# A retention front moved off GpSimd, with scores on array quarters and small products on array halves

## The chip, the cores and the metric

The kernel runs on one NeuronCore of a Trainium2 chip. The metric is the device time of one execution in microseconds (us). Three runs of the kernel before gave 735.53, 735.69 and 737.09 us, median 735.69 us; this kernel's measurement can tell about 0.2% from no change. The engines are named as in the profile: PE (TensorE, matrix products), PEld (its weight loads), DVE (VectorE), ACT (ScalarE), POOL (GpSimd) and SP (SyncE, which here only starts transfers).

## The reference, cut to what matters

Three layers follow each other, all in fp32.

```python
# 1 retention: batch 2, heads 8, sequence 768, head width 64
state = gamma[h] * state + outer(k_t, v_t)        # gamma differs by head
y_t   = scale * (q_t @ state)                     # -> x: 1536 tokens x 512

# 2 mixture of 8 experts, one expert per token, at most `capacity` = 384 tokens each
expert = argmax(x @ w_gate, axis=1)
pos    = number of earlier tokens of the same expert
out[i] = gate_w[i] * relu(x[i] @ w1[expert]) @ w2[expert]     if pos < capacity, else 0

# 3 four experts that every token passes, weighted by normalised domain_probs
out = sum_e p[:, e] * (relu(x @ w1[e]) @ w2[e])
```

## The kernel before, in words

The kernel has a front (layer 1 and the routing of layer 2), then the products of layer 2, then those of layer 3. The change lies wholly in the front, which ends with the first expert product (line 950). All work is written out in program order; each engine takes its own instructions strictly in that order, and semaphores hold an instruction until what it reads is there and what it overwrites has been read.

The front works on 12 token tiles of 128 tokens (6 per batch entry), numbered 0 to 11 here. For a tile i it does:

- `st_v`: vg(i) = v times a decay factor per head and position, 128x512, on POOL (line 250). It needs the transfer kv(i).
- `st_S`: the scores S(i) = k q, 8 products of 64 rows and 128 columns (line 266), into two PSUM banks, then on DVE the causal mask, giving sd(i) (line 271).
- `st_I`, `st_U`, `st_O`: products with the carried state (line 309), the new state U (line 290, copied out by ACT, line 295), and the scores times vg (line 321). `st_I` and `st_O` add up in the same two banks.
- `st_x`: O(i) is copied out by ACT (line 335) and multiplied by the decay `gqs` on POOL (line 336) into xT(i), the tokens with features on partitions. For the last two tiles DVE does both in one step (line 340).
- `x_pe`: the token product X(i) (line 364), 4 products against `iw`, an identity with the gate's 8 columns beside it: this turns the tile to one token per partition and gives the gate logits at once. `x_reduce` then has DVE add up the logits (line 379), ACT copy the tokens out to `xk` (line 383), and ACT's queue write `xk` to DRAM, `xd` (line 387).
- `x_dve`: the argmax as a one-hot `ohs`, the running counts `cum`, and `ohk` (token number times one-hot), all small DVE instructions.
- `r_pe`, `r_dve`: the rank product R(i) (lines 349, 350) counts earlier tokens of the same expert; DVE picks the token's rank and makes the selection matrix `at` (line 439, 128x256).
- `g_pe`: the selection product (line 446) collects the token numbers per expert slot.

A loop over `it` from 0 to 11 sets the order: it does `st_I/U/O/x` of tile it-1, `st_v` of tile it+1, `st_S` of tile it, starts the transfers of tile it+3 (512 KB each for q with k, and for k with v; 256 KB of `gqs` in the first rounds), then `x_pe` of tile it-2, `g_pe` of it-4, `r_pe` of it-3. "Round it" below is one pass of this loop. At round 8 the first expert weight is split in two (`split_w(0)`: ACT line 141, then DVE line 142). After the loop stand the last tiles' remaining steps, the gather of the first expert's tokens, and products (lines 528, 536) that build its input.

PSUM has eight banks: four are handed out in turn to S, O and R, and four are fixed (`slot` for the selection, `u` for the state, `x0` and `x1` for the token product).

## Time and profile before

| | before |
|---|---|
| median of 3 runs | 735.69 us |
| profiled execution | 735.49 us, span 733.7 us, granted clock 0.999 |
| PE busy over the span | 722.3 us (98%) |
| DVE, ACT, POOL busy | 473.5, 339.0, 202.5 us |
| first expert product (line 950) starts | 68.46 us after the span's start |

The span runs from the first to the last instruction of the profiled execution; some 1.8 us of its own time lie around it. After 70 us PE is busy without a gap in every stretch, so the time of the front stands ahead of a rigid block. "PE busy" counts matmuls whose ends are modelled and overlap, so how dense PE really works is read from where the next group starts. Products of fp32 stand in the trace as two instructions each. [...]

### The profile page before, as it was taken

What the parts mean: (1) busy time and instruction counts of PE and PEld (TensorE: products, weight loads), DVE (VectorE), ACT (ScalarE), POOL (GpSimd) and SP (SyncE); (2) the same over time, 40 slices, a digit from 0 to 9 for tenths busy, and PEclk for the clock granted to TensorE, in tenths of its full rate; (3) what the DMA queues carried; (4) which work ended last, traced back from release to release, by engine and by line L of the source; (5) the groups of instructions that cost most, each with busy time, mean ns of one, the idle gap of its engine ahead of it and who ended that gap; (6) DMA issues with size and microseconds to landing.
All of it is one profiled execution on the core that took longest, in us unless ns stands there. A gap on an engine that the chain in (4) does not pass through costs nothing.

```text
span 733.7 us, 11338 instructions
## 1 busy us (share of the span) xinstructions
PE 722.3 (98%) x4425; PEld 657.2 (90%) x4426; DVE 473.5 (65%) x777; ACT 339.0 (46%) x545; POOL 202.5 (28%) x193
## 2 busy tenths in 40 slices
PE   8998999999999999999999999999999999999997
PEld 6887999999999888999889998889998899988896
DVE  3888899898898835545743655763475454557334
ACT  2344767676656533334433445633344334444331
POOL 3653854443044012212323111223422121111103
PEclk9999999999999999999999999999999999999999
DMA  9984886687741211211122122122222212112102
GB/s 331 414 338 138 287 320 220 228 281 245 230 144 34 89 55 59 86 58 58 61 91 78 38 77 87 59 85 88 87 72 71 92 53 86 59 58 79 37 1 86
DMA packets 28026, 92.83 MB, mean 127 GB/s; under 512 B 4097, under 2 KB 4369, under 8 KB 27970
## 3 DMA queue, kind: packets, MB, share of 16 engines
q1 hardware_dynamic: 23042, 81.79, 32.2%
q0 software_dynamic: 3056, 7.05, 2.8%
q10 hardware_dynamic: 1872, 3.24, 1.2%
q8 instruction: 35, 0.57, 0.3%
q14 instruction: 21, 0.17, 0.1%
HBM read 85.72 MB, written 6.34 MB: 125 GB/s over the span
## 4 chain that ended last, share of the span: by engine, by line
PE 88%; DVE 1%; POOL 1%; ACT 0%; issue 0%; POOLq 0%; ACTq 0%
PE o L1212 35%; PE a L1056 17%; PE m L950 15%; PE b L1056 9%; PE m L953 7%; PE bb L1056 5%; POOL out_dram L1224 1%; PE ab L1056 0%; DVE x L855 0%; DVE X L868 0%; ACT X L864 0%; DVE c L1149 0%; POOLq L1409 0%; ACT c L1087 0%; PE T L768 0%
## 5 line engine op out<-in xcount | busy, mean ns | idle before, releaser
L1212 PE MATMUL o<-w,g_c 128*128 128x512 f32 x1152 | 267.4, 390 | 0.0
L1212 PEld LDWEIGHTS o<-w,g_c 128*128 128x128 f32 x1152 | 215.9, 188 | 43.7
L142 DVE TENSOR_TENSOR w<-raw,w 128x1024 fp32r<-128x1024 f32 x128 | 158.4, 1247 | 13.9 <-ACT w L141 13.6
L1056 PE MATMUL a<-X,w 128*128 128x384 f32 x720 | 145.2, 336 | 0.0
L157 POOL TENSOR_TENSOR t<-raw 128x512 f32<-128x512 f32 x28 | 38.8, 1386 | 349.6 <-DMA raw<-b 302.2
L1091 DVE TENSOR_TENSOR c<-b,c 128x384 f32<-128x384 f32 x30 | 16.7, 558 | 181.1 <-PE b L1056 181.1
L141 ACT CAST w<-raw 128x1024 fp32r<-128x1024 f32 x128 | 132.1, 1047 | 2.5 <-DMA raw<-a 1.1
L1056 PEld LDWEIGHTS a<-X,w 128*128 128x128 f32 x720 | 127.5, 188 | 2.6 <-DVE c L1091 0.3
L1087 ACT COPY c<-a 128x384 f32<-128x384 f32 x60 | 28.8, 479 | 196.3 <-PE a L1056 196.3
L950 PE MATMUL m<-xet,w 128*128 128x448 f32 x256 | 80.8, 375 | 0.8 <-PEq L635 0.8
L1072 ACT ACTIVATE g_c<-c 128x384 fp32r<-128x384 f32 x96 | 50.4, 526 | 66.0 <-DVE c L1091 64.7
L950 PE MATMUL m<-h,w 128*128 128x448 f32 x256 | 80.8, 375 | 0.0
L1056 PE MATMUL b<-X,w 128*128 128x384 f32 x360 | 72.1, 334 | 0.0
L953 PE MATMUL m<-h,w 128*128 128x224 f32 x256 | 67.5, 264 | 0.0
L953 PE MATMUL m<-xet,w 128*128 128x224 f32 x256 | 67.5, 264 | 0.0
L624 POOL DMA_INDIRECT xe<-xd,gidx x42 | 53.7, 1278 | 47.3 <-DVE xT L752 35.7
L1056 PEld LDWEIGHTS b<-X,w 128*128 128x128 f32 x360 | 63.5, 188 | 0.0
L1076 DVE SCALAR_TENSOR_TENSOR g_c<-c,g_c 128x384 fp32r<-128x384 f32 x96 | 52.9, 552 | 3.9
L950 PEld LDWEIGHTS m<-xet,w 128*128 128x128 f32 x256 | 48.0, 187 | 4.6 <-PEq L635 1.0
L950 PEld LDWEIGHTS m<-h,w 128*128 128x128 f32 x256 | 48.0, 187 | 3.7
L953 PEld LDWEIGHTS m<-xet,w 128*128 128x128 f32 x256 | 48.9, 191 | 0.0
L953 PEld LDWEIGHTS m<-h,w 128*128 128x128 f32 x256 | 48.9, 191 | 0.0
(158 smaller groups left out, 766.7 us busy)
## 6 DMA issues: line engine op xcount, KB each, us to landing
raw<-a SPq DMA_DIRECT2D x64, 512.0 KB, 4.9
raw<-b SPq DMA_DIRECT2D x64, 512.0 KB, 3.5
qk<-qkv SPq DMA_DIRECT2D x12, 512.0 KB, 8.3
kv<-qkv SPq DMA_DIRECT2D x12, 512.0 KB, 8.1
xd<-xk ACTq DMA_DIRECT2D x12, 256.0 KB, 6.2
gqs<-gqt SPq DMA_DIRECT2D x6, 256.0 KB, 7.5
xe<-xd,gidx POOLq DMA_INDIRECT x44, 4.9
iw<-cst SPq DMA_DIRECT2D x1, 272.0 KB
```

The lines of the kernel that those rows point to most:

```text
L141: nc.scalar.copy(w[:, 0], r)
L142: nc.vector.tensor_tensor(out=w[:, 1], in0=r, in1=w[:, 0].bitcast(F32), op=ALU.subtract)
L157: eng.tensor_tensor(out=c[:, 0:2], in0=b[:, 2:4], in1=b[:, 1:3], op=sub)
L624: nc.gpsimd.indirect_dma_start(out=t[:, b], out_offset=None, in_=xq, in_offset=bass.IndirectOffsetOnAxis(ap=gidx[:, b, e:e + 1], axis=0),)
L950: nc.tensor.matmul(out=b2, lhsT=w[0], rhs=x, start=first, stop=last, skip_group_check=True)
L953: nc.tensor.matmul(out=b2[:, 0], lhsT=w[1], rhs=x[:, 0], start=False, stop=last, skip_group_check=True)
L1056: nc.tensor.matmul(out=bk[:, 0:HT], lhsT=w[:, sw, k], rhs=x[:, sx, k], start=(first and m == 0), stop=(m == len(steps) - 1), skip_group_ch ...
L1072: nc.scalar.activation(out=h2[:, 0], in_=src, func=AF.Relu)
L1076: nc.vector.scalar_tensor_tensor(out=h2[:, 1], in0=src, scalar=0.0, in1=h2[:, 0].bitcast(F32), op0=ALU.max, op1=ALU.subtract,)
L1087: nc.scalar.copy(t, bk[:, 0:HT])
L1091: nc.vector.tensor_tensor(out=t, in0=bk[:, 0:HT], in1=t, op=ALU.add)
L1212: nc.tensor.matmul(out=bk, lhsT=h2[:, sh, cols], rhs=w[:, sw, k], start=(q == 0 and m == 0 and (n, t) not in begun), stop=(m == 2), skip_g ...
```

## The change

- POOL leaves the front, except for vg(0) and vg(1). The other ten vg are made by ACT, in 8 instructions of 128x64 each, at the place in the program where POOL's stood. xT is made by DVE for all tiles, straight from PSUM. `ohk` moves from DVE to ACT.
- The scores are 16 products on 64x64 quarters of the array in place of 8 on 64x128. From round 4 on they stand at the head of the round, ahead of `st_I`.
- The token, rank and selection products are cut in halves of 64 array columns: 8, 4 and 4 products a round in place of 4, 2 and 2. The rank product writes into the spare end of the token product's bank and stands ahead of it.
- PSUM is dealt out in pairs of banks: one for S (`s2`), one for O (`o2`), one for X with R (`x`). The ring of four is gone.
- The logits are added up in one DVE instruction, the maximum is a second; `xk` is one ACT copy of 512 columns in place of two of 256. The selection compares against an fp16 table.
- The constant `iw` is no longer loaded whole (544 columns): an identity and the gate (160 columns) are loaded after kv(2), and ACT spreads them. kv(1) is started ahead of gq(0), kv(2) ahead of the constants.
- The steps after the loop stand in another order.

```diff
+    def two(tag, name):
+        return ps[0].tile([P, 2, 512], F32, tag=tag, name=name)
...
         def st_v(i):
...
+            v = kv[:, 1].rearrange("p (h d) -> p h d", h=8)
+            if i < 2:
+                nc.gpsimd.tensor_tensor(
...
+            else:
+                for h in range(8):
+                    nc.scalar.activation(
+                        out=vg[:, h], in_=v[:, h], func=AF.Copy, scale=gk[:, i % NCH, h:h + 1]
+                    )
...
         def st_S(i):
...
-            bks = [bank(f"S{i}_{j}") for j in range(2)]
+            s2 = two("s2", f"S{i}")
+            bks = [s2[:, j] for j in range(2)]
             for hp in range(4):
                 cols = slice(hp * P, (hp + 1) * P)
-                for j in range(2):
+                for m in range(4):
+                    o, j = 64 * (m >> 1), m & 1
                     r = slice(64 * j, 64 * j + 64)
                     nc.tensor.matmul(
-                        out=bks[j][:, cols], lhsT=qk[r, 1, cols], rhs=qk[r, 0, cols],
-                        start=True, stop=True,
+                        out=bks[j][o:o + 64, cols],
+                        lhsT=qk[r, 1, hp * P + o:hp * P + o + 64], rhs=qk[r, 0, cols],
...
         def st_x(i):
...
-            if i < NT - 2:
-                ot = p2.tile([P, 512], F32, tag="ot", name=f"ot{i}")
-                for j in range(2):
-                    nc.scalar.copy(ot[:, 256 * j:256 * j + 256], bks[j][:, 0:256])
-                nc.gpsimd.tensor_tensor(out=xT, in0=ot, in1=gqs[:, c], op=ALU.mult)
...
+            for j in range(2):
+                cols = slice(256 * j, 256 * j + 256)
+                nc.vector.tensor_tensor(
+                    out=xT[:, cols], in0=bks[j][:, 0:256], in1=gqs[:, c, cols], op=ALU.mult
+                )
...
+        def r_pe(i, bk):
+            for o in (0, 64):
+                half = bk[o:o + 64]
+                nc.tensor.matmul(
+                    out=half, lhsT=onesb[:, o:o + 64], rhs=cum[:, i], start=True, stop=False,
...
+        def x_pe(i, rank=None, reduce=True):
...
+            b2 = xbs[i] = two("s2" if i == NT - 1 else "x", f"X{i}")
+            if rank is not None:
+                r_pe(rank, b2[:, 1, 448:456])
+            for hp in range(KD):
+                for o in (0, 64):
+                    nc.tensor.matmul(
+                        out=b2[o:o + 64, hp // 2, hp % 2 * 256:hp % 2 * 256 + 136],
+                        lhsT=xT[:, hp * P + o:hp * P + o + 64], rhs=iw[:, hp], start=True,
...
-            yield nc.vector.tensor_scalar(
-                out=ohk[:, i], in0=ohs[:, i], scalar1=tok[:, i:i + 1], scalar2=None, op0=ALU.mult
+            yield nc.scalar.activation(
+                out=ohk[:, i], in_=ohs[:, i], func=AF.Copy, scale=tok[:, i:i + 1]
             )
...
         for it in range(NT):
+            if it >= EARLY_S:
+                st_S(it)
             if it >= 1:
                 st_I(it - 1)
...
-            st_S(it)
+            if it < EARLY_S:
+                st_S(it)
...
+            if it == 1:
+                eye = ig[:, 0:P].rearrange("p (k c) -> p k c", k=1).to_broadcast([P, KD, P])
+                nc.scalar.copy(iw[:, :, 0:P], eye)
+                nc.scalar.copy(iw[:, :, P:136], ig[:, P:XW].rearrange("p (k c) -> p k c", k=KD))
...
-                x_pe(it - 2)
+                x_pe(it - 2, it - 3 if it >= 3 else None)
...
         st_I(NT - 1)
-        x_pe(NT - 2)
-        r_pe(NT - 3)
         st_O(NT - 1)
-        braid(r_dve(NT - 3))
-        g_pe(NT - 4)
-        g_pe(NT - 3)
         st_x(NT - 1)
+        x_pe(NT - 2, NE - 1, False)
+        g_pe(NE - 2)
+        braid(r_dve(NE - 1))
+        g_pe(NE - 1)
```

On ACT, in round 2 of the kernel before, from the state copy of tile 1 to the write of tile 0's tokens (`ot` is the copy of O(1), `xk` that of X(0)):

```order
L295 COPY st_114<-U_173 128x256
L335 COPY ot_244<-O_0_216 128x256
L335 COPY ot_244<-O_1_217 128x256
L383 COPY xk_270<-X_0_272 128x2x4x32
L383 COPY xk_270<-X_1_273 128x2x4x32
L387 DMA xd<-xk_270 128x512
```

The same place on ACT in the changed kernel (`kv_178` is the transfer kv(3)):

```order
L311 COPY st_116<-U_181 128x256
L265 ACTIVATE vg_267<-kv_178,cdec 128x64 x8
L397 COPY xk_304<-X_305 128x4x4x32
L401 DMA xd<-xk_304 128x512
L423 ACTIVATE ohk<-ohs,kc 128x8
```

The eight instructions that need kv(3) now stand ahead of the copy that empties X(0)'s banks; before they stood on POOL's queue.

On PE, in the kernel before, from the last score product of round 5 to the first state product of round 6 (`S` are scores, `O` what `st_I` and `st_O` write, `slot_ps` the selection):

```order
L266 MATMUL S_1_490<-qk_263 128x128
L364 MATMUL X_0_509<-iw,xT_398 128x136 x2
L364 MATMUL X_1_510<-iw,xT_398 128x136 x2
L446 LDWEIGHTS at_449
L446 MATMUL slot_ps<-ohk,at_449 128x8
L446 LDWEIGHTS at_449
L446 MATMUL slot_ps<-ohk,at_449 128x8
L349 LDWEIGHTS onesb
L349 MATMUL R_523<-cum,onesb 128x8
L350 LDWEIGHTS ub
L350 MATMUL R_523<-ohs,ub 128x8
L309 MATMUL O_0_537<-qk_263,st_115 64x128
```

On PE in the changed kernel, round 5 from its start up to its token product:

```order
L281 MATMUL S_515<-qk_296 64x128 x16
L326 MATMUL O_534<-qk_231,st_116 64x128 x8
L306 MATMUL U_181<-vg_354,kv_234 64x64 x8
L338 MATMUL O_534<-sd_417,vg_354 64x128 x8
L361 LDWEIGHTS onesb
L361 MATMUL X_579<-cum,onesb 64x8
L365 LDWEIGHTS ub
L365 MATMUL X_579<-ohs,ub 64x8
L361 LDWEIGHTS onesb
L361 MATMUL X_579<-cum,onesb 64x8
L365 LDWEIGHTS ub
L365 MATMUL X_579<-ohs,ub 64x8
```

The scores went from between O and X to the head of the round, next to the state product that also uses quarters, and the rank product went ahead of X into X's own tile.

## Rows read from the trace of the kernel before

**Rows 1.** Busy us (instructions) of PE, PEld, DVE, ACT, POOL; granted clock, DMA share, GB/s.

```profile
40.00:50.00 10.00, 10.00 (x168) 8.88 (x167) 8.28 (x33) 4.68 (x13) 4.83 (x5) 1.00 1.03 415
...
70.00:80.00 10.00, 10.00 (x68) 9.59 (x67) 8.60 (x13) 6.14 (x12) 7.87 (x8) 1.00 0.86 286
```

**Rows 2.** The chain that ended last, 0 to 70 us: start, length, what.

```profile
67.88 0.58 issue
68.46 0.44 PE m L950
```

**Rows 3.** Timeline of PE, a round: start, length, line, op, out<-in.

```profile
42.16 0.67 PE L309 MATMUL O<-qk,st 64*64 64x128 f32 x16
42.76 0.69 PE L290 MATMUL U<-vg,kv 128*64 128x64 f32 x16
43.28 1.10 PE L321 MATMUL O<-sd,vg 128*64 128x128 f32 x16
44.30 1.16 PE L266 MATMUL S<-qk 64*128 64x128 f32 x16
45.40 1.19 PE L364 MATMUL X<-iw,xT 128*128 128x136 f32 x8
46.43 0.20 PE L446 MATMUL slot_ps<-ohk,at 128*128 128x8 f16 x2
46.48 0.17 PE L349 MATMUL R<-cum,onesb 128*128 128x8 f16 x1
...
46.60 0.32 PE L309 MATMUL O<-qk,st 64*64 64x128 f32 x1
```

**Rows 4.** Timeline of PE, rounds 3 and 4.

```profile
17.70 1.16 PE L266 MATMUL S<-qk 64*128 64x128 f32 x16
18.79 1.19 PE L364 MATMUL X<-iw,xT 128*128 128x136 f32 x8
...
22.23 1.16 PE L266 MATMUL S<-qk 64*128 64x128 f32 x16
23.32 1.20 PE L364 MATMUL X<-iw,xT 128*128 128x136 f32 x8
```

**Rows 5.** Timeline of POOL: vg(2), vg(3), vg(4); in brackets the idle time before.

```profile
15.05 1.04 POOL L250 TENSOR_TENSOR vg<-kv,cdec 128x512 f32<-128x512 f32 x1 [3.01 <-DMA kv<-qkv]
...
19.59 1.04 POOL L250 TENSOR_TENSOR vg<-kv,cdec 128x512 f32<-128x512 f32 x1 [2.26 <-PE X L364]
...
22.93 1.04 POOL L250 TENSOR_TENSOR vg<-kv,cdec 128x512 f32<-128x512 f32 x1 [1.06 <-DMA kv<-qkv]
```

**Rows 6.** Groups by line and form, 0 to 56 us: busy, mean ns | idle before.

```profile
L383 ACT COPY xk<-X 128x256 f32<-128x256 f32 x19 | 6.2, 375 | 17.1 <-DVE lgs L379 17.1
...
L397 DVE SCALAR_TENSOR_TENSOR cd<-lgs,mxs,kc 128x8 f32<-128x8 f32 x9 | 4.5, 496 | 0.3
...
L446 PEld LDWEIGHTS <-at 128*128 128x128 f16 x16 | 1.6, 98 | 0.1
...
L141 ACT CAST w<-raw 128x1024 fp32r<-128x1024 f32 x1 | 1.0, 1045 | 0.9 <-DMA kv<-qkv 0.9
```

**Rows 7.** Timeline of PE, the scores of round 7.

```profile
35.31 1.16 PE L266 MATMUL S<-qk 64*128 64x128 f32 x14 [0.35 <-DVE ranks L424]
```

**Rows 8.** Timeline of DVE, rounds 8, 9 and after.

```profile
44.95 1.23 DVE L142 TENSOR_TENSOR w<-raw,w 128x1024 fp32r<-128x1024 f32 x1 [0.79 <-ACT w L141]
46.09 1.28 DVE L271 TENSOR_TENSOR sd<-S,cdec 128x512 f32<-128x512 f32 x2
...
53.52 0.76 DVE L340 TENSOR_TENSOR xT<-O,gqs 128x256 f32<-128x256 f32 x2
...
56.29 0.23 DVE L397 SCALAR_TENSOR_TENSOR cd<-lgs,mxs,kc 128x8 f32<-128x8 f32 x1
```

**Rows 9.** Timeline of PE, after the loop.

```profile
54.49 1.19 PE L364 MATMUL X<-iw,xT 128*128 128x136 f32 x8
...
68.46 0.44 PE L950 MATMUL m<-xet,w 128*128 128x448 f32 x1 [0.83 <-PEq L635]
```

More of the change, by code (lines that the diff above doesn't have):

```diff
@@ L75, in tile_retention_moe_moe, with one, bank @@
     ps = [sctx.enter_context(tc.tile_pool(name="ps", bufs=1, space=PSUM))]
-    banks = [f"bank{n}" for n in range(4)]
-    held = ["slot", "u", "x0", "x1"]
+    pairs = ["s2", "o2"]
     nbank = [0]
-    def bank(name, tag=None):
-        if tag is None:
-            tag = banks[nbank[0] % len(banks)]
-            nbank[0] += 1
+    def two(tag, name):
+        return ps[0].tile([P, 2, 512], F32, tag=tag, name=name)
+    def one(tag, name):
         return ps[0].tile([P, 512], F32, tag=tag, name=name)
+    def bank(name):
+        nbank[0] += 1
+        return two(pairs[nbank[0] % 2], name)[:, 0]
     def warm(n, fill):
@@ L282, in st_U @@
             if c == 0:
[L283 removed]
+                u_ps[0] = one("u", f"U{i}")
             u = u_ps[0][:, 0:KD * HD].rearrange("p (a d) -> p a d", a=KD)
@@ L302, in st_I @@
             c = i % NCH
-            live[i]["o"] = [bank(f"O{i}_{j}") for j in range(2)]
+            o2 = two("o2", f"O{i}")
+            live[i]["o"] = [o2[:, j] for j in range(2)]
             q = live[i].pop("q")
@@ L369, in x_pe @@
             if reduce:
                 x_reduce(i)
[L372 removed]
         def x_reduce(i):
[L375 removed]
             xk = xks[i]
[L377 to L386 removed]
+            b3 = xbs.pop(i).rearrange("p g (q c) -> p (g q) c", q=2)
@@ L387, in x_reduce @@
+            nc.vector.tensor_reduce(
+                out=lgs[:, i], in_=b3[:, :, P:136].rearrange("p k e -> p e k"), axis=AX.X,
+                op=ALU.add,
+            )
+            nc.scalar.copy(
+                xk.rearrange("p (b k c) -> p k b c", b=4, k=KD),
+                b3[:, :, 0:P].rearrange("p k (b c) -> p k b c", b=4),
+            )
             nc.scalar.dma_start(out=xd[1 + i * P:1 + (i + 1) * P], in_=xk)
-            nc.vector.tensor_tensor_reduce(
-                out=lgs[:, i], in0=lgs[:, i], in1=part, scale=1.0, scalar=-FMAX, op0=ALU.add,
-                op1=ALU.max, accum_out=mxs[:, i],
-            )
+            nc.vector.tensor_reduce(out=mxs[:, i], in_=lgs[:, i], axis=AX.X, op=ALU.max)
@@ L445, in g_pe @@
             for b in range(SL // P):
-                nc.tensor.matmul(
-                    out=slot_ps[:, b], lhsT=at[:, b * P:(b + 1) * P], rhs=ohk[:, i],
-                    start=(i == 0 and b == 0), stop=True, skip_group_check=True,
-                )
+                for o in (0, 64):
+                    nc.tensor.matmul(
+                        out=slot_ps[o:o + 64, b], lhsT=at[:, b * P + o:b * P + o + 64],
+                        rhs=ohk[:, i], start=(i == 0 and b == 0), stop=True,
+                        skip_group_check=True,
+                    )
         def braid(*seqs):
@@ L498, in tile_retention_moe_moe, with late, fetched @@
                 split_w(0)
+        k01, k23 = range(2), range(2, KD)
+        def late(i, ks):
+            for k in ks:
+                nc.tensor.matmul(
+                    out=xt0[k // 2][:, k % 2], lhsT=xks[i][:, k * P:(k + 1) * P], rhs=at0[i],
+                    start=(i == NE and k % 2 == 0), stop=True, skip_group_check=True,
+                )
+        def fetched(ks):
+            for b in range(SL // P):
+                w = min(SM - b * P, P)
+                for k in ks:
+                    nc.tensor.matmul(
+                        out=xt0[k // 2][:, k % 2, b * P:b * P + w],
+                        lhsT=xe0[:, b, k * P:(k + 1) * P], rhs=ident[:, 0:w],
+                        start=False, stop=True, skip_group_check=True,
+                    )
         st_I(NT - 1)
-        x_pe(NT - 2)
-        r_pe(NT - 3)
         st_O(NT - 1)
-        braid(r_dve(NT - 3))
-        g_pe(NT - 4)
-        g_pe(NT - 3)
         st_x(NT - 1)
+        x_pe(NT - 2, NE - 1, False)
+        g_pe(NE - 2)
+        braid(r_dve(NE - 1))
+        g_pe(NE - 1)
         nc.vector.tensor_copy(gidx0, slot_ps[:, :, 0])
@@ L549, in tile_retention_moe_moe @@
         slot_at(NT - 1)
-        late(NE + 1)
+        late(NT - 1, range(KD))
         g_pe(NT - 2)
         g_pe(NT - 1)
-        for b in range(SL // P):
-            fetched(b, range(2))
+        fetched(k01)
         nc.vector.tensor_scalar(
@@ L572, in tile_retention_moe_moe @@
         nc.vector.tensor_copy(rows, slot_ps.rearrange("p b e -> p (b e)"))
-        rps = bank("rows", "u")[:, 0:NB4 * E1]
+        rps = one("u", "rows")[:, 0:NB4 * E1]
         for b in range(NB4):
@@ L579, in tile_retention_moe_moe @@
             )
-        for b in range(SL // P):
-            fetched(b, range(2, KD))
+        fetched(k23)
     def offsets():
```

131 lines of the change are left out of this document (48 added, 83 removed).

## The prediction

> **What bounds the kernel now.** The views were read in this order. First the busy time by stretches: after 70 us PE is busy for 10.00 of 10 us [rows 1], so what comes behind the front moves as one piece, and a microsecond won or lost in the front is one in the total. Then the chain that ended last: read back from the end it is expert products all the way to 68.46 us [rows 2]. So the question is when that product can start. Then PE's timeline inside the front. In an undisturbed round each group of products follows the one before without a wait, 4.44 us from 42.16 to 46.60 [rows 3]: PE sets the pace there. The stretches show a second bound beside it: from 10 to 50 us the transfers run at a share of 1.03 and some 415 GB/s [rows 1], so each tile's data lands when the queue lets it, and the early rounds wait for it: POOL sat idle for kv(2) until 15.05 and for kv(4) until 22.93 [rows 5]. The reader is to see two limits close together: transfers in the first rounds, PE in the later ones.
>
> **The change part by part.** The sum has four terms, made against the profiled execution (735.49 us, 0.20 under the median).
>
> *First term, the early rounds: +2.1 us.* In the changed order, ACT's queue holds vg(3) ahead of the copy of X(0) out of its banks, and X now has one pair of banks, so R(0) and X(1) cannot start before that copy. vg(3) needs kv(3). Its landing has no row of its own. It lies before 19.59, where POOL took it up, and between kv(2) at 15.05 and kv(4) at 22.93 [rows 5]. Each round moves 1.31 MB, 3.2 us at 415 GB/s [rows 1], which puts it between 18.3 and 19.6. I take 19.4, nearer the later bound, since its own row is the nearest. Loading the identity once saves 384 columns of 128 rows of 4 bytes, 0.20 MB or 0.5 us: 18.9. Starting kv(2) earlier only reorders transfers that are all ahead of kv(3).
>
> vg on ACT: no row shows eight small instructions. From 256 to 1024 columns ACT's time grows from 375 to 1045 ns [rows 6], 0.87 ns a column and some 0.15 fixed. How far the fixed parts overlap no row here shows: the ends are 0.6 (one instruction of 512) and 1.7 (eight times 0.21), and I take the middle, 1.1. The copy of 512 columns takes 0.6 by the same slope. With 0.2 of semaphores and the rank product ahead, X(1) starts at 18.9 + 1.1 + 0.6 + 0.3 = 20.9. Before, it started at 18.79 [rows 4], when PE had done the same work, S(3) included. That is +2.1, from +1.2 to +3.0 with the ends of vg and of the landing. From round 4 on S stands first in the round; a round then has the same pieces in another order, which by itself moves nothing. Later transfers don't bind again: vg(4) would follow kv(4) at 22.4, so X(2) could start at 24.4, and PE gets there at 25.1.
>
> *Second term, the rounds: -0.19 us each.* [...] Before, the form changes four times in a round; now S and I share quarters and the rest shares halves, so it changes twice. [...] The small products are 8 in place of 4. Before, two of them take 0.05 [rows 3]; four more at that spacing cost 0.10, and I take 0.08 to 0.10. A round is then 4.25, with ends at 4.10 (changes cost more than I see) and 4.45 (halves load slower).
>
> From X(2) at 23.32 [rows 4] to X(9) at 54.49 [rows 9] are 31.17 us for seven rounds. At 4.44, less the missing U(5) and I(6) (0.5 and 0.6), they would be 30.0: 1.2 us are stalls. Those come from POOL: the small DVE step `cd` takes 0.23 when POOL is idle [rows 8] and 0.496 in the mean [rows 6], and the scores of round 7 wait for DVE [rows 7]. With POOL gone from the rounds I count them at nothing. After: 7 x 4.25 - 1.0 = 28.8. The step from X(1) to X(2) is 4.25 in place of 4.53. Together -0.3 - 2.4 = -2.7.
>
> *Third term, a new wait in round 8: +0.7 us.* DVE's work per round is the mask 1.28, xT 0.76 (new in ten of the rounds) and some 1.4 of small steps, 3.5 of 4.25: it fits. But at round 8 DVE also waits for the weight split on ACT and does its 1.23 part [rows 8]. Before, the next scores had other banks to go to. Now S has one pair, and S(10) waits until sd(9) is read, behind that split. 1.23 plus the wait, less 0.75 of slack in DVE's round, leaves about 0.7; from 0 to 1.2.
>
> *Fourth term, after the loop: -0.3 us.* From X(9) to the first expert product are 13.97 us [rows 9], a chain that alternates between PE and DVE through two selections. Leaving DVE are three `ohk`, three second reductions and part of two selection tables; the maximum becomes a step of its own, and the gather's index stands ahead of tile 10's reduction. I count -0.3, from -1.0 to +0.5.
>
> Moved at no cost: `ohk` on ACT (busy 4.68 of 10 us in the stretch shown of the front [rows 1]) and the two copies that spread the identity, which end before X(1) matters; X(0) starts up to a microsecond later for them, and that is hidden in the wait for kv(3). If kv(3) came early, it would show.
>
> The sum: +2.1 - 2.7 + 0.7 - 0.3 = -0.2, so 735.3 for a profiled execution and 735.5 on the median.
>
> **The rivals.**
>
> *The early wait is not there (faster).* If X(1) starts before 19.6, because kv(3) lands a microsecond earlier in the new order or ACT's eight instructions are short, the rounds' gain stays: 735.5 - 1.9 = 733.6. For it: 15.05 and one round of transfers give a landing of 18.3. Against it: kv(4) at 22.93 less one round gives 19.7 [rows 5].
>
> *The small products in halves are slow (slower).* They stand on PE's path, eight weight loads and eight products a round. If each load's 98 ns [rows 6] lay open, they would take 0.8 in place of 0.2, +0.6 in each of nine rounds, +5; half open, +2.4, so 737.9. It decides once they cost over 0.16 a round more than I count. Against it: before, their 98 ns loads are hidden and two take 0.05 [rows 3]. [...] No run so far shows an fp16 load of 64 columns. [...]
>
> *The transfers bound the whole front (no change).* Then nothing but the 0.5 us of the smaller constant could be won, 735.2. For it: the share of 1.03 until 50 us [rows 1]. Against it: in the round shown [rows 3] PE waits for nothing, and X(1) is the only product that I find held by a landing.
>
> **How the numbers follow.** Forecast (early loss and later gain cancel) 0.53, with its own range 734.2 to 736.8. Early wait absent, 0.25. Small products slow, 0.19. Transfers, 0.03. 0.2% is 1.5 us: faster means under 734.2, slower over 737.2. The forecast's ends put a little on either side: faster 0.26, same 0.53, slower 0.21. The range for 8 in 10 reaches from the first rival's time, 733.5, to 737.7, most of the half-open case. Predicted 735.5.
>
> **What would show it.** Right: in the new profile R(0) and X(1) start near 20.9 with ACT's copy as releaser; two scores in later rounds lie 4.2 to 4.3 us apart; no DVE step is stretched; S(10) waits for DVE; X(9) starts within a microsecond of 54.5. Wrong: X(1) before 19.6, a round above 4.45 with gaps around the rank or selection products, or a front in which PE is released by transfers after round 4.

## The result, and the profile after

The changed kernel takes 743.49 us (median of 4 runs, 743.00 to 744.69), the kernel before 735.62 beside it (735.53 to 737.09): a ratio of 1.0109, 95% interval 1.0096 to 1.0122. It is 1.1% slower. The prediction, 735.5 with a range from 733.5 to 737.7, was wrong by 8 us.

The profiled execution has a span of 741.4 us against 733.7. Three places in it cut the 7.7 us into four pieces:

| stretch | before | after | difference | forecast |
|---|---|---|---|---|
| start to X(1) | 18.79 | 21.26 | +2.5 | +2.1 |
| X(1) to X(9) | 35.70 | 35.21 | -0.5 | -2.0 (rounds -2.7, wait in round 8 +0.7) |
| X(9) to the first expert product | 13.97 | 16.70 | +2.7 | -0.3 |
| from there to the end of the span | 665.2 | 668.2 | +3.0 | 0 |

In the table X(9) is the token product of tile 9, the last one inside the loop.

*First piece.* ACT's and PE's timelines of the changed kernel (start, length, engine, line, operation, out<-in; in brackets the idle time before and what ended it), which answer to [rows 4, 5]:

```profile
18.67 2.02 ACT L265 ACTIVATE vg<-kv,cdec 128x64 f32<-128x64 f32 x8 [2.53 <-DMA kv<-qkv]
20.60 0.56 ACT L397 COPY xk<-X 128x512 f32<-128x512 f32 x1
```
```profile
15.93 1.15 PE L382 MATMUL X<-iw,xT 128*64 128x136 f32 x16 [1.67 <-ACT iw L493]
...
19.14 1.10 PE L281 MATMUL S<-qk 64*64 64x128 f32 x32
21.20 0.20 PE L361 MATMUL X<-cum,onesb 128*64 128x8 f16 x2 [0.96 <-ACT xk L397]
```

The chain is the one forecast: kv(3), vg(3), the copy of X(0), R(0). kv(3) lands a little earlier than I put it, and the eight vg instructions take 2.02 us, not 1.1. A second delay shows in PE's first line: X(0) waits 1.67 us for the copies of the identity, and starts at 15.93 instead of 13.86.

*Second piece.* PE's timeline, an undisturbed round and two later places, against [rows 3]:

```profile
26.81 1.10 PE L281 MATMUL S<-qk 64*64 64x128 f32 x32 [0.20 <-PE X L382]
27.70 0.65 PE L326 MATMUL O<-qk,st 64*64 64x128 f32 x16
28.28 0.69 PE L306 MATMUL U<-vg,kv 128*64 128x64 f32 x16
28.79 1.10 PE L338 MATMUL O<-sd,vg 128*64 128x128 f32 x16
...
30.68 0.26 PE L458 MATMUL slot_ps<-ohk,at 128*64 128x8 f16 x4
30.87 1.10 PE L281 MATMUL S<-qk 64*64 64x128 f32 x32
...
34.47 1.66 PE L281 MATMUL S<-qk 64*64 64x128 f32 x32
...
41.12 0.44 PE L326 MATMUL O<-qk,st 64*64 64x128 f32 x6 [0.94 <-issue]
...
47.10 0.99 PE L338 MATMUL O<-sd,vg 128*64 128x128 f32 x14 [0.75 <-issue]
```

The round is 4.06 us, 0.38 below the 4.44 of before and 0.19 below the forecast. But within S(7), I(7) and O(8) PE stands for 0.5 to 0.9 us in the middle of a group, with "issue" as the reason: nothing that the profile knows is waited for. PE's busy time is modelled; counted by where the next group starts, the three places cost 0.6, 1.4 and 1.0 us. From X(2), at 25.39, to X(9) are 31.08 us. Seven rounds of 4.06 without the U(5) and I(6) that are missing would be 27.3, so 3.7 us are stalls, where the kernel before had 1.2. That gives all of the gain of these seven rounds back; what is left of the second piece is the step from X(1) to X(2), 4.13 instead of 4.53.

*Third and fourth piece.* Behind the loop GpSimd gathers the rows of expert 0's tokens. PE turns them in two groups of eight products (the fetched groups, line 535, into `T0x`), ACT rounds the result to a high part (the cast into `xet`), DVE subtracts that to get the low part, and the first expert product reads both. Ahead of it stands a branch at which every engine jumps over a part of the program, the one for experts with more tokens than their 224 slots; it isn't needed with these inputs. First the kernel before (PE, ACT, DVE), then the changed one, from the gather on:

```profile
66.51 1.11 PE L536 MATMUL T0x<-ident,xe 128*128 128x128 f32 x8
66.54 0.53 ACT L783 CAST xet<-T0x 128x448 fp32r<-128x448 f32 x1 [3.13 <-PE T0x L536]
67.10 0.62 DVE L787 TENSOR_TENSOR xet<-T0x,xet 128x448 fp32r<-128x448 f32 x1 [1.10 <-ACT xet L783]
```
```profile
62.32 1.15 POOL xe L551
...
63.77 4.86 DMA xe<-xd,gidx
...
69.52 0.98 PE T0x L535 x8
70.50 0.02 issue
70.53 0.54 ACT xet L805
71.07 1.33 issue
72.40 0.64 DVE xet L809
73.03 0.14 issue
73.17 0.71 PE m L972
```

The second is the chain that ended last (start, length, what). The last fetched group starts 12.9 us behind X(9) (12.0 before), and the product 3.8 behind the group (1.95 before). ACT's cast now waits for the whole group (70.53; before it starts beside it). DVE's subtraction has its data at 71.07 and starts at 72.40. And the clock, against [rows 1] (busy us and instructions of PE, PEld, DVE, ACT, POOL, then granted clock, DMA share, GB/s):

```profile
60.00:70.00 10.00, 7.90 (x86) 6.66 (x81) 6.25 (x36) 2.65 (x5) 2.12 (x2) 1.00 0.44 134
70.00:80.00 10.00, 7.32 (x32) 6.73 (x31) 5.40 (x14) 4.75 (x7) 5.79 (x6) 0.66 0.50 164
80.00:90.00 10.00, 10.00 (x68) 9.58 (x67) 8.16 (x11) 6.95 (x12) 5.77 (x5) 1.00 0.56 184
```

At the end of a wait of 2.68 us the granted clock of TensorE was 0.50 (half clock below), from 71.9 to 78.7 us: 0.66 in the mean of the stretch from 70 to 80 us, with products of 0.60 and 0.39 us instead of 0.38 and 0.27.

### The profile page after: what moved, and what is told of

The parts are those of the page before. It is cut to its first block, busy times and chain, and to the rows that moved or that the text cites. A ratio compares the mean times of both kernels' runs of the same rounds, so it can differ in the third digit from the quotient of the medians.

```text
span 741.4 us, 12013 instructions
## 1 busy us (share of the span) xinstructions
PE 723.8 (98%) x4761; PEld 659.3 (89%) x4762; DVE 467.7 (63%) x762; ACT 354.5 (48%) x607; POOL 180.2 (24%) x173
## 4 chain that ended last, share of the span: by engine, by line
PE 92%; DMA 3%; DVE 1%; issue 1%; ACT 1%; POOL 1%; SPq 0%; POOLq 0%; ACTq 0%
PE o L1234 35%; PE a L1078 17%; PE m L972 15%; PE b L1078 8%; PE m L975 7%; PE bb L1078 5%; PE X L382 1%; PE S L281 1%; DMA kv<-qkv 1%; PE O L338 1%; DMA gqs<-gqt 1%; DMA xe<-xd,gidx 1%; PE U L306 1%; POOL out_dram L1246 1%; PE O L326 1%
## 5 line engine op out<-in xcount | busy, mean ns | idle before, releaser
L146 DVE TENSOR_TENSOR w<-raw,w 128x1024 fp32r<-128x1024 f32 x128 | 156.4, 1232 | 14.5 <-ACT w L145 13.3
L972 PE MATMUL m<-xet,w 128*128 128x448 f32 x256 | 83.4, 383 | 2.7 <-DVE xet L809 2.7
L646 POOL DMA_INDIRECT xe<-xd,gidx x42 | 52.2, 1243 | 53.2 <-DVE xT L774 37.6
L972 PEld LDWEIGHTS m<-xet,w 128*128 128x128 f32 x256 | 49.3, 193 | 6.8 <-issue 2.8
L975 PEld LDWEIGHTS m<-xet,w 128*128 128x128 f32 x256 | 50.1, 196 | 0.0
```

The costliest lines, as they stand in the source:

```text
L146: nc.vector.tensor_tensor(out=w[:, 1], in0=r, in1=w[:, 0].bitcast(F32), op=ALU.subtract)
L646: nc.gpsimd.indirect_dma_start(out=t[:, b], out_offset=None, in_=xq, in_offset=bass.IndirectOffsetOnAxis(ap=gidx[:, b, e:e + 1], axis=0),)
L972: nc.tensor.matmul(out=b2, lhsT=w[0], rhs=x, start=first, stop=last, skip_group_check=True)
L975: nc.tensor.matmul(out=b2[:, 0], lhsT=w[1], rhs=x[:, 0], start=False, stop=last, skip_group_check=True)
```

## The experiments

All start from the changed kernel. Behind each time stands its ratio to the kernel before on the same chip, with the 95% interval. The parts of the trace are from one execution of each.

**Stalls of PE, 256 instructions apart.** The stalls lie at TensorE's records 1218, 1474 and 1730 of the trace (products, weight loads and what its sequencer does, counted together), 256 apart. The page of the profile lists transfers of instructions by queue (packets, MB, share of time); on q8 they are, before and after:

```profile
q8 instruction: 35, 0.57, 0.3%
```
```profile
q8 instruction: 38, 0.62, 0.3%
```

In the trace each has 16,384 bytes; those on the other queue of instructions, q14, have 8,192 from 1 us on.

The first run shifts them, by 96 instructions ahead of X(0) (shortened):
```
+ for _ in range(48): matmul(out=dm[:, 0, 0:8], lhsT=fill[:, 0:P], rhs=fill[:, 0:8])
```


> The changed kernel with 48 added tiny fp16 products (96 instructions on TensorE, 8 columns each, result not used) just ahead of X(0), where TensorE waits 1.67 us anyway; nothing else differs. Theory A: TensorE's stalls at S(7), I(7) and O(8) lie 256 instructions apart because a block of TensorE's instructions arrives late; with 96 more instructions ahead of them they move 96 instructions earlier in the program, about half a round: to O or the X behind it in round 7, to S(8) or the X before it, and to I, U or the scores of round 9, and the time stays within 1 us of 743.5. Rival B: they are waits for data of those very groups; then S(7), I(7) and O(8) stay the ones that are stretched.

744.30 us, 1.0118 (1.0102 to 1.0133). PE's timeline at the stalls:

```profile
28.66 0.54 PE L281 MATMUL S<-qk 64*64 64x128 f32 x10 [0.81 <-issue]
...
34.20 0.44 PE L326 MATMUL O<-qk,st 64*64 64x128 f32 x4 [0.40 <-issue]
...
40.49 0.33 PE L382 MATMUL X<-iw,xT 128*64 128x136 f32 x1 [0.19 <-issue]
...
46.77 0.56 PE L281 MATMUL S<-qk 64*64 64x128 f32 x12 [1.16 <-issue]
```

They moved to other groups, S, I, X and S: the groups that hold records 866, 1122, 1378 and 1634 of the changed kernel, 96 ahead of 962, 1218, 1474 and 1730. This is theory A. The place in the instruction stream decided, not the data. The transfers fit: at each of the three stalls of the changed kernel one of 16,384 bytes on q8 had begun 2.20 to 2.40 us before PE went on (32.64 to 35.04 us, 38.88 to 41.12 and 44.90 to 47.10). Not every such place has a stall. At record 962 of the changed kernel, where the transfer had begun 2.65 us earlier (26.36 to 29.01), there is none, and none at 1986 and 2242, which PE reaches at 52.5 and 57.8 us, when the transfers' share is 0.31 (50 to 60 us). That the busy queues make a block of instructions late is my reading and not shown: no run took the other transfers away.

The next run has fewer instructions, by scores on halves (shortened):
```
- for m in range(4): o, j = 64 * (m >> 1), m & 1; out=bks[j][o:o+64, cols], ...
+ for j in range(2): out=bks[j][:, cols], lhsT=qk[r, 1, cols], rhs=qk[r, 0, cols]
```


> The changed kernel with the score products on array halves as before (16 products of 64 rows and 128 columns a tile instead of 32 of 64 by 64): 176 instead of 208 instructions a round on TensorE; nothing else differs. Theory A (TensorE's instructions come in blocks of 256 and arrive late when TensorE takes them fast): a block lasts 1.45 instead of 1.23 rounds, and the stalls of TensorE between 30 and 50 us, some 2.2 us in three places, shrink to 1 us or less; an undisturbed round, 4.06, gets 0.1 to 0.2 longer since S and I no longer share the array's form. X(9) 0 to 1 us earlier, 742.5 to 743.5 us. Rival B: the quarters are worth nothing, and a round stays 4.06; X(9) then 1 to 1.5 us earlier, 742 us. Rival C: the number of instructions doesn't matter, the stalls keep their size, and rounds get longer: 744 to 745 us.

743.50 us, 1.0093 (1.0078 to 1.0109). No such stall is left from 30 to 46 us:

```profile
38.06 1.16 PE L280 MATMUL S<-qk 64*128 64x128 f32 x16
...
42.37 1.16 PE L280 MATMUL S<-qk 64*128 64x128 f32 x16
...
47.80 0.94 PE L280 MATMUL S<-qk 64*128 64x128 f32 x12 [1.07 <-issue]
```

A round is 4.31 (38.06 to 42.37), so the quarters are worth 0.25 of it. S(10) now waits 1.07 us, for sd(9), which ends at 47.70 behind DVE's weight split: the third term of the prediction. In the changed kernel the stall of O(8) covers most of it, and S(10) waits 0.23 us. X(9) starts at 55.23, 1.2 us earlier, a little more than theory A has it; the products on tile 10's tokens then run at half clock (1.76 us for a group that takes 0.99; granted clock 0.83 from 60 to 70 us), and the gain is gone.

The third has fewer by leaving the token, rank and selection products undivided (`for o in (0, 64)` taken out of three helpers):

> The changed kernel with the token, rank and selection products undivided as before (128 array columns): 184 instead of 208 instructions a round on TensorE; the scores stay on quarters; nothing else differs. Theory A (blocks of 256 instructions that arrive late): the stalls of TensorE between 30 and 50 us, 2.2 us in three places, shrink to 1 us or a little more, while a round gets up to 0.2 us longer, since array forms change twice more: X(9) within 0.7 us of 56.5, 743 to 744 us. Rival B: the halves do nothing for a round (4.06 stays): X(9) 1 us earlier, 742.5 us. Rival C: the halves are what makes rounds shorter than forecast (4.06 against 4.25): a round is 4.25 or longer, X(9) later than 57 us, 744 to 745 us.

743.12 us, 1.0095 (1.0079 to 1.0110). One stall of 0.39 is left between 30 and 46 us; the round 38.37 to 42.59 is 4.22. This is theory A: the halves are worth 0.16 a round. X(9) starts 0.9 us earlier, and half clock on tile 10's products (1.83 us for that group) takes that back, as in the run before.

**The early wait.** Here vg of a round stands behind the copy of X (shortened):
```
- st_v(it + 1)  (behind st_x(it - 1))
+ st_v(it + 1)  (behind x_pe(it - 2, ...))
```


> The changed kernel with ACT's eight vg instructions of a round put behind the copy of X out of its banks instead of ahead of it, from tile 3 on; nothing else differs. Theory A: vg(3) (landing at 18.6 plus 2.0 us on ACT) is what holds R(0) and X(1) back; X(1) then starts near 19.3 instead of 21.26, later rounds come up to 1.9 us earlier as far as the transfers let them, and the kernel takes 741.6 to 742.5 us. Rival B: the transfers, or TensorE's own stalls, take the gain back: X(1) early but X(9) within 0.3 us of 56.5, 743.5 us.

743.72 us, 1.0106 (1.0090 to 1.0121). R(0) starts at 20.12 directly behind S(3), 1.1 us earlier; PE itself is late by the rest, for X(0). The gain is lost again, at the stalls of I(7) and O(8) and in round 8: vg now stands ahead of the weight split on ACT, for which DVE waits, and S(10) waits 1.55 us for DVE.

```profile
41.15 0.45 PE L326 MATMUL O<-qk,st 64*64 64x128 f32 x7 [1.18 <-issue]
44.13 1.10 PE L281 MATMUL S<-qk 64*64 64x128 f32 x32
47.41 1.10 PE L338 MATMUL O<-sd,vg 128*64 128x128 f32 x16 [1.13 <-issue]
51.11 1.10 PE L281 MATMUL S<-qk 64*64 64x128 f32 x32 [1.55 <-issue]
```

**The clock.** Eight products on zeros fill part of PE's wait, ahead of the branch:
```
  fetched(k23)
+ warm(8, fill)
```


> The changed kernel with 8 added fp16 products of 512 columns on zeros (their result is not used) on TensorE behind the last fetched group and ahead of the branch; nothing else differs. Theory A: the half clock behind 71.7 us follows from TensorE's idle stretch of 2.7 us; with 1.7 us of it filled, the granted clock stays 1.0 in the stretch from 70 to 80 us, the first expert product stays at 73.2 us, and the kernel takes about 741.0 us (-2.5). Rival B: the half clock comes from something else than TensorE's own idleness; it stays, and the time too, 743.5 us.

741.64 us, 1.0075 (1.0061 to 1.0089). The profiled execution has a granted clock of 1.00 from 70 us on, with 1.19 us of the wait for DVE still there. From the first expert product to the end it takes 665.8 us (739.9 less 74.06) instead of 668.2. So the half clock is worth 2.4 us here, and it went with PE's own standing still, 2.68 us against 1.19, since nothing else was changed.

```profile
70.00:80.00 10.00, 8.81 (x62) 7.36 (x58) 5.94 (x15) 4.91 (x8) 4.90 (x6) 1.00 0.48 161
```

**DVE behind the branch.** The first run puts the casts and subtractions (the splits) ahead of the branch:

> The changed kernel with the split of expert 0's tokens (two casts on ACT, two subtractions on DVE) and the index table put ahead of the branch on the overflow instead of behind it; nothing else differs. Theory A: behind the branch DVE's next instruction comes late because its instructions are not there yet (4.25 us put down to issue), which delays the first expert product by 1.8 us; TensorE then idles for 2.7 us and gets half the clock, another 2.5 us. Then the first expert product starts some 2 us after the fetched group (71.4 instead of 73.17), no half clock is granted behind 71 us, and the kernel takes about 739.2 us. Rival B: the subtraction waits for data (the casts or the gathered rows), and its place beside the branch is immaterial: first expert product at 73.2, 743.5 us. In between: the wait goes and the half clock stays, 741.7 us.

743.61 us, 1.0099 (1.0083 to 1.0114). The wait only changed its place: PE's first product, at 74.42, is released by DVE's leaving the branch, behind the second split and the index table. But the run answers rival B. With no branch ahead of it the subtraction starts with the end of its cast:

```profile
71.62 0.53 ACT L762 CAST xet<-T0x 128x448 fp32r<-128x448 f32 x1 [5.72 <-PE T0x L535]
```
```profile
72.19 0.62 DVE L766 TENSOR_TENSOR xet<-T0x,xet 128x448 fp32r<-128x448 f32 x1 [3.39 <-ACT xet L762]
```

So DVE does not lack data, and its lateness goes with the branch.

The second run puts the gather of expert 1 behind the splits (`gidx1` and `load_rows(1, gidx1)` moved there):

> The changed kernel with the row index of expert 1 (a small cast on DVE) and its gather on GpSimd put behind the four splits of expert 0's tokens; nothing else differs. In the changed kernel GpSimd works on that gather from 71.33 to 72.29 and DVE's subtraction starts at 72.40, 1.34 behind the cast that it needs. Theory A: DVE can't start a subtraction while GpSimd works on the gather. Then the subtraction starts within 0.1 us of the cast's end, the first expert product comes 1.3 us earlier against the fetched group, TensorE idles 1.4 instead of 2.7 us, and the time is 742.2 us if the half clock stays, 739.8 if it goes too. Rival B: behind the branch DVE's instructions themselves come late, whatever GpSimd does: the subtraction stays 1.1 to 1.6 us behind the cast, 743.5 us.

748.38 us, 1.0171 (1.0157 to 1.0185). GpSimd is idle until 75.88, and DVE's subtraction is as late as ever, 1.46 behind its cast (71.58 to 73.04). Theory A is wrong. The kernel gets slower, since the first expert product now starts at 75.10, 5.2 us behind the last fetched group, released by the cast that was moved.

The third has two tiles in place of one (shortened):
```
- x2p = two("x", "T0x");  xt0 = [x2p[:, g, ...] for g in range(2)]
+ xt0 = [two(("x", "o2")[g], f"T0x{g}")[:, 0, ...] for g in range(2)]
```


> The changed kernel with expert 0's transposed tokens in two tiles of one bank each, in two pairs of banks, instead of one tile of two banks (the rotating banks of the warm-up and of the overflow part, which does not run, become one pair); nothing else differs. Theory A: ACT's first cast waits for all fetched groups because both halves are one tile; with two tiles it starts behind the first half, at about 69.5 instead of 70.53, and the first subtraction behind it at 70.1 comes ahead of GpSimd's gather too. First expert product some 1.8 us behind the second fetched group (71.2 instead of 73.17): 741.5 us if the half clock stays, 739.2 if it goes. Rival B: DVE's instructions come 3.2 us behind the branch whatever they wait for: product at 73.2, 743.5 us.

743.28 us, 1.0093 (1.0078 to 1.0108). The first half of A holds: ACT's cast starts at 68.92, beside the group of 68.90. The second does not: DVE starts at 72.25 all the same.

```profile
72.25 1.16 DVE L811 TENSOR_TENSOR xet<-T0x,xet 128x448 fp32r<-128x448 f32 x2 [4.39 <-ACT w L145]
```

In these runs the subtraction comes 3.3 to 3.4 us behind DVE's branch (69.14 to 72.40, 69.66 to 73.04, 68.86 to 72.25), whatever it needs. The delay is not a constant, though. Behind the end of its cast the subtraction starts by 1.34, 1.46 and 2.80 us in these three, and by 1.58 with the products on zeros, 1.07 with vg behind the copy and 1.10 with the shifted instructions; DVE's idle time ahead of it is 4.25, 4.45 and 4.39, then 4.30, 4.12 and 3.57. The next run shifts DVE's instructions, by 64 memsets of one column ahead of the first scores:

> The changed kernel with 64 added memsets of one column on DVE in its idle time ahead of the first scores; nothing else differs. They shift every later DVE instruction by 64 places. Theory A: DVE's instructions behind the branch come late because the place where it goes on lies near the end of a block of instructions, and the next block is fetched only then (instruction transfers of 8 KB stand in the trace around it, 3.3 us from branch to subtraction in the changed kernel, in the one with the gather moved and in the one with two tiles). Shifted by 64, the subtraction follows the branch within 2 us: first expert product 1 to 1.3 us earlier against the fetched group, 742.3 us with the half clock, 740 without. Rival B: any jump costs DVE 3.3 us here, wherever its instructions lie: subtraction 3.2 to 3.4 us behind the branch again, 743.5 us.

742.00 us, 1.0083 (1.0068 to 1.0097). The memsets take 8.16 us and delay the front, and half clock comes twice (granted clock 0.69 from 10 to 20 us, 0.83 from 70 to 80); but the subtraction, at 73.03, is released by its cast, after 2.89 us of idle time. Then 64 memsets that are jumped over:

> The changed kernel with 64 memsets on DVE put at the head of the overflow part, which is jumped over: nothing more is executed, but all that DVE executes behind the branch lies 64 instructions further on. Theory A (the place behind the jump lies at the edge of a block of instructions): DVE's subtraction starts within 0.1 us of the cast it needs, the first expert product comes 1.3 us earlier against the fetched group; 742.2 us if the half clock stays, 739.8 if it goes. Rival B: what helped the run with the executed memsets was something else that they shifted, such as the time at which DVE comes to the branch: subtraction 1.1 to 1.6 us behind its cast, 743.5 us.

On a chip where the kernel before took 740.59: 745.82 us, 1.0065 (1.0040 to 1.0090). The subtraction comes at 72.37, 1.31 behind its cast and after 4.26 us of idle time, about as before (1.34 and 4.25), so 64 places behind the jump change nothing. Then 11 executed memsets:
```
  braid(*seqs)
+ if it < 11: nc.vector.memset(offs[:, 0, 0:1], 0.0)
```


> The changed kernel with 11 added memsets of one column on DVE, one in each of the first 11 rounds, where DVE has slack; nothing else differs. DVE then comes to the branch with as many recorded instructions behind it as in the kernel before (202 to its first branch instruction; the changed kernel has 191). Theory A: whether DVE's instructions behind the branch are there in time depends on where the branch stands in DVE's blocks of instructions; then the subtraction follows its cast by 0.1 to 0.5 us, the first expert product comes 0.9 to 1.3 us earlier against the fetched group, 742.2 us with the half clock, 739.8 without. Rival B: 11 places do not matter (64 executed ones did, 64 jumped-over ones did not): 3.2 to 3.4 us from branch to subtraction again, 743.5 us or up to 0.3 more.

740.56 us, 1.0066 (1.0053 to 1.0079): with eleven useless instructions the kernel takes some 3 us less. DVE, then PE:

```profile
70.83 0.62 DVE L811 TENSOR_TENSOR xet<-T0x,xet 128x448 fp32r<-128x448 f32 x1 [3.23 <-ACT xet L807]
```
```profile
69.11 1.11 PE L537 MATMUL T0x<-ident,xe 128*128 128x128 f32 x8
71.60 0.44 PE L974 MATMUL m<-xet,w 128*128 128x448 f32 x1 [1.37 <-DVE xet L811]
```

The subtraction follows its cast (70.80), after 3.23 us of idle time. The product stands 2.5 us behind the fetched group instead of 3.8, PE stands still for 1.4 us, and the granted clock is 1.00 from 70 to 80 us in the profiled execution. That a block of DVE's instructions is fetched late is my reading and not shown. In the changed kernel a transfer of 8,192 bytes on q14 begins at 70.54, 1.86 us ahead of the subtraction, and another at 70.88, but the trace doesn't tell which engine a transfer is for. That the number of executed instructions decides rests on this one run. The run with 64 is hardly a second one: there the cast released the subtraction only at 73.03, so DVE can have been late up to then.

**Putting it back together.** The first run changes what stands behind the loop: two tiles, the splits ahead of the branch, and 5 products on zeros.

> The changed kernel with three edits behind the loop and none ahead: expert 0's transposed tokens in two tiles of one bank, their four splits ahead of the branch (the index table stays behind it), and 5 fp16 products of 512 columns on zeros, not used, behind the last fetched group. Theory A: the cast starts behind the first half of the fetched groups, DVE has nothing on the path behind the branch, and TensorE doesn't idle over 1.5 us: first expert product 2.6 us behind the second fetched group instead of 3.8, no half clock behind 70 us, 740.0 us (739.4 to 740.8). Rival B: TensorE's first product still waits for DVE to pass the branch, and the 3.3 us that DVE's next instructions are late show in the third weight block's split instead: products stall a few us later and the gain is the clock's alone, 741.2 us.

739.96 us, 1.0056 (1.0043 to 1.0069), in A's range for the total, with the product 3.0 behind the group: PE waits 0.82 for DVE's branch, as B has it. The second changes the front: scores on halves, vg behind the copy of X, DVE's part of the weight split a round later, the copies of the identity (`iw`) ahead of vg(2).

> The changed kernel with its front altered and the rest as it was: scores on array halves again (176 instead of 208 TensorE instructions a round), ACT's vg of a round behind the copy of X, the two copies of the identity ahead of vg(2), and DVE's part of the first weight split one round later than ACT's. Theory A: X(0) starts at 14.4 instead of 15.9 and X(1) near 18.8 instead of 21.26, no block of TensorE's instructions is late, the scores of tile 10 wait less than 0.6 us, and X(9) starts at 53.0 to 54.0 instead of 56.49; 740 to 741 us. Rival B: the transfers hold the early rounds (tile 5's scores can't start before 23.2, its values land at 25.1): X(1) early, but X(9) at 54.7 or later, 742 to 742.5 us.

739.11 us, 1.0052 (1.0039 to 1.0065). X(0) starts at 14.29 as expected, then I(2) waits 1.03 for the state copy behind vg(2), and X(1) comes at 19.79; X(9) at 54.14 lies between the two theories. The third has both together:

> The front of the run above and the tail of the run before it together. Theory A: both gains add up, 736 to 738.5 us, so at best equal to the kernel before (735.7); the rest of the loss is in the chain between X(9) and the first expert product. Rival B: an earlier front leaves TensorE idle for longer ahead of the gathered rows, and half clock comes in there: 739 us or more.

737.63 us, 1.0028 (1.0015 to 1.0040): theory A. The fourth run has this front with the state copy first, two tiles, the jumped-over memsets and the splits behind the branch ("the sum run" below); the fifth adds tile 10's reduction ahead of the gather:

> The altered front (scores in halves, vg behind the copy of X, DVE's part of the weight split a round later), with the copies of the identity and vg(2) one round later in ACT's queue so that the state copy of tile 1 stands ahead of them; expert 0's tokens in two tiles; the 64 jumped-over memsets. The splits stay behind the branch, no products are added. Theory A: tile 2's first products start at 15.4 instead of 16.5, X(1) near 18.9, X(9) at 53.3, the fetched group 13.0 behind it, the first expert product 1.4 to 1.9 behind that (68.0), no half clock: 734.5 us, 1 under the kernel before. Rival B: half clock behind 60 us all the same, 736.5 to 738 us. Rival C: with this front the place behind the jump is at an edge again, product 3.8 behind the fetched group, 738 us.

> The run above with tile 10's reduction and copy put ahead of the gather instead of behind it, as the kernel before has it. In the changed kernel GpSimd's gather starts 0.87 us behind its index, at the end of ACT's copy of X(10), in the kernel before 0.29 behind it. Theory A: the gather waits for that copy; with the copy earlier it follows its index by 0.3 us, while DVE's index comes up to 0.35 later: gather and fetched group 0.2 to 0.6 us earlier, 734.2 us. Rival B: the gather waits for something else (the landing of the last rows it may read): no change, 734.5 us, or 0.3 slower for the later index.

On the chip of 740.59: 741.96 us, 1.0022 (1.0012 to 1.0032), and 742.19, 1.0021 (1.0011 to 1.0032). Both miss theory A's gain. In the first X(1) starts at 19.03 as expected, X(9) at 54.05 (53.3 expected, S(10) still waits), DVE is late (70.06, after 4.33 us of idle time, rival C), and half clock follows (granted clock 0.83 from 70 to 80 us). In the second the gather starts 0.87 us behind its index as before, though the copy had ended at 58.71, 1.9 us earlier: ACT's copy, which the profile of the changed kernel names as releaser, does not hold it. In the changed kernel, too, the gather comes 0.87 behind the index, in the kernel before 0.29. What holds it stays open; GpSimd had been idle for 47.9 us in the changed kernel and for 7.7 before. The last two runs have a memset a round and both weight splits behind the loop, without and with 5 products on zeros in PE's waits there:

> The sum run with three differences: no jumped-over memsets but one executed memset a round in twelve rounds; DVE's part of the first weight split behind the loop, next to the second one, so that the scores of tile 10 don't wait for it; the two small casts for the row indices ahead of these splits. Theory A: X(9) 1 us earlier than in the sum run (53.0), fetched group at 66.2, DVE in time behind the branch, first expert product at 67.7 or a little later, no half clock: 0.3% under the kernel before. Rival B: DVE is 3.3 us late behind the branch again: equal to the kernel before or 0.2% over it. Rival C: half clock in the chain behind the loop: 0.2 to 0.5% over it.

> The run above with 5 added fp16 products of 512 columns on zeros, not used, in two of TensorE's waits behind the loop (2 ahead of the last selection product, 3 ahead of the products on tile 10's tokens). Theory A: they cost nothing (the waits are 0.55 and 0.82 us) and keep the clock at 1.0 from 55 to 75 us: equal to the run above where that shows no half clock, 1.7 to 3.4 us faster where it does. Rival B: they delay the chain by up to 0.5 us, or the half clock comes all the same.

Without them 738.96 us, 1.0039 (1.0026 to 1.0052), with a granted clock of 0.83 from 60 to 70 and from 70 to 80 us; with them 736.32, 1.0015 (1.0004 to 1.0025), and 1.00 in both stretches of the profiled execution:

```profile
57.74 0.60 PE L567 MATMUL dm<-fill 128*128 128x512 f16 x2
...
60.08 0.82 PE L587 MATMUL T0x<-fill 128*128 128x512 f16 x3
...
66.69 1.11 PE L554 MATMUL T0x<-ident,xe 128*128 128x128 f32 x8
69.25 0.44 PE L998 MATMUL m<-xet,w 128*128 128x448 f32 x1 [1.45 <-DVE xet L835]
```

The run with the five products takes 2.6 us less than the run with half clock. Two of the twelve executions still took 739.5 and 739.9 us, with a mean granted clock of 0.995 instead of 0.998 to 1.0. In both runs the weight splits stand ahead of DVE's branch, and the first expert product waits 1.96 and 1.45 us for DVE's subtraction, 2.68 in the changed kernel. With most of the causes taken away the loss falls from 1.09% to 0.15%. No version beats the kernel before.

## Why the prediction was wrong

Of the 8 us, 3.0 lie in the fourth term, 3.0 behind the first expert product, where the forecast was 0, 1.5 in the rounds and 0.4 in the first term.

- *First term, +2.1, came out at +2.5.* Wait, place and releaser are right. The size is off: "vg on ACT, 1.1" measured 2.02, above the upper end of 1.7. The slope from wide instructions hid what a short one costs on its own: one of 64 columns lasts 336 ns in the mean of 80 in the front of the changed kernel, where the slope gave 210, and neighbours overlap, so that eight take 2.02. That the term came out near is partly luck: 0.8 too little for vg stands against 0.5 too much for the landing and for what follows the copy. The 0.2 for semaphores was my estimate, and no run shows it: R(0) starts 0.04 us behind the end of the copy (21.16) and X(1) 0.10, where the forecast had 0.3. The identity's copies cost X(0) not "up to a microsecond" but 2.1 us. That is hidden in the changed kernel, as forecast, but not without the wait for vg: with vg out of the way R(0) came only 1.1 us earlier.
- *Second term, rounds of 4.25: better than forecast, 4.06.* The quarters are worth 0.25 of a round and the halves 0.16. The forecast takes 0.27 off the 4.44 for S and X; that came from an array time for each group that no run shows. Measured from group to group, S takes 0.89 instead of 1.10 and X 0.95 instead of 1.03, together 0.29 less. The part not forecast lies in O, which takes 0.88 instead of 1.02, and 1.03 in the run with X undivided behind it. That the changes of the array's form are what was saved is my estimate; no run separates them from the smaller pieces. The small products took the 0.25 us a round that I counted. Their loads of 64 fp16 columns take 110 ns, 98 for 128 columns before, and are hidden, so the rival "small products in halves are slow" did not happen.
- *"With POOL gone from the rounds I count them [the stalls] at nothing" is the step that failed here: 3.7 us of stalls.* The small DVE steps are no longer stretched (cd 0.23 in the rounds shown). But 208 instead of 152 instructions a round bring new stalls of PE, 2.9 us of the 3.7, while the transfers run at a share of 1.0. I took 64-column pieces as a matter of array time alone and never counted instructions.
- *Third term, +0.7 in round 8.* The wait is there: 1.07 in the run with scores on halves, mostly covered by a stall in the changed kernel.
- *Fourth term, -0.3, measured +2.7, and with what follows it +5.7: the largest miss.* I counted DVE's steps and stopped at "a chain that alternates between PE and DVE". The steps up to the gather's index did get shorter, by 0.1 us. What failed is that I took the rest of the chain as unchanged. The gather starts 0.6 us later behind its index. The last fetched group starts another 0.4 later, and PE waits for the rows ahead of it. One tile of two banks makes the cast wait for the whole group (1.1 us), and DVE starts late behind the branch (1.3); the two cost 1.8 together, since before PE's own branch ended last. And with PE's longer wait, 2.68 us, comes the half clock (2.4). The tile stood in the diff (`x2p = two("x", "T0x")`); the others could not be read off it. Shown by runs are the tile, the link of DVE's lateness to the branch, and the clock; the cause of the gather's delay is open.
- "After 70 us ... what comes behind the front moves as one piece" holds to 0.1% here only at equal clock: 665.2 before, 665.3 to 666.1 in the runs with a mean granted clock of 0.998 or 0.999, 668.2 after. This is the other step that failed: the front's waits also set the clock of what follows.

## What to carry to other kernels

Where a product is cut into pieces for the array's sake, count instructions as well as columns: here TensorE, at 51 instructions per us beside transfers at a share of 1.0, stood for up to 1.2 us at places 256 instructions apart in its stream. Make a tile no larger than what its first reader needs: with one tile of two banks the cast waited for both halves and started at 70.53, with two tiles at 68.92. And a wait ahead of a dense stretch can cost twice, once by itself and once in clock: 2.4 us of half clock came with 2.7 us of wait here, and products on zeros in the wait bought the second part back.

## What had not been expected of the hardware

- TensorE stood for up to 1.2 us at places 256 instructions apart, at 51 instructions per us with a transfer share of 1.0; at 41 per us (176 in 4.31) it did not from 30 to 46 us. At the three stalls of the changed kernel a transfer of 16,384 bytes of instructions had begun 2.20 to 2.40 us before it went on.
- DVE's first instruction behind a branch started 1.07 to 2.80 us behind the end of the cast that it reads in seven runs. With 11 more instructions executed ahead of the branch it started 0.03 behind it in the one run that tried it.
- A round of the same columns took 4.06 us with scores on quarters ahead of other products on quarters, and 4.31 with scores on halves.
